# Tokens in groups of 1024 instead of 512: one scan, decay, sigmoid and product over two PSUM banks, late expert weights, late constants

## The chip, the cores and the metric

The kernel runs on one core of one Trainium2 chip. The metric is the device time of the kernel in microseconds (us). The kernel before takes 220.52 us, the median of three runs (220.2 to 220.78). Engines are called by the names of the profile: PE is the matrix engine (TensorE), PEld its weight load, DVE is VectorE, ACT is ScalarE, POOL is GpSimd, SP is SyncE, which here only issues DMAs.

A run is called slow here when it took over 1.5% longer than the fastest run of the same kernel; the others are fast. Ratios compare fast runs with fast runs, and profiles are of fast runs, unless the text says otherwise. A median is of all runs of a kernel.

## The reference, cut to what matters

```python
# x, f_logit: (4, 5056, 256) float32; lower_bound: (256,)
sig = 1 / (1 + np.exp(-f_logit))
f = lower_bound + (1 - lower_bound) * sig
for t in range(S):                       # a recurrence over 5056 tokens, per batch and channel
    h = f[:, t] * h + (1 - f[:, t]) * x[:, t]
    y[:, t] = h
# y as (20224, 256) goes into a soft mixture of 8 experts with 4 slots each
logits = y @ phi                         # phi: (256, 32)
d = softmax(logits, axis=0)              # over all 20224 tokens
slot_in = d.T @ y                        # 32 slots
slot_out[e] = relu(slot_in[e] @ w1[e]) @ w2[e]    # w1: 256 x 1024, w2: 1024 x 256
out = softmax(logits, axis=1) @ slot_out
```

The last line needs the slots of all tokens. So no output can start before the whole input has been scanned, and the kernel has three stages: an input stage (load, gate, scan, logits, slot sums), a short expert stage, and an output stage. The profile counts 58.2 MB read from HBM and 20.7 MB written.

## The kernel before: the parts that matter

A unit is 512 tokens of one batch, and four units (one of each batch) are a group. 5056 tokens are nine groups of 512 and one of 448, which lies on 112 partitions.

```python
R = 4; G = P * R                          # 4 tokens a partition, 512 a unit
def rows(g): return min(P, (S - g * G) // R)
# ... constants: identities, phi scaled by (1 - lower_bound), all before the loop ...
W_AT = {i: 1 for i in range(1, 34, 4)}    # which unit issues how many of the 16 weight loads
W_AT.update({34: 1, 35: 2, 36: 2, 37: 2})
# pools: ld 6 (f_t, x_t), sup 4 (s_t, u_t), apool 6 (decays), hpool 7,
# PSUM: psu 2 (sp and up, one bank each), ptp 1 (hp), plg 1 (logits, two banks), pslot 1

def load(n):      # f_t and x_t, 512 KB each, by nc.sync.dma_start
    ...
    nc.sync.dma_start(out=fs[n][:n_p], in_=f_logit[b, ds(g * G, n_p * R)]...)
def gate(n):      # ACT: s = sigmoid(-f_logit), bf16
    nc.scalar.activation(sts[n][:n_p], fs.pop(n)[:n_p], ACT.Sigmoid, scale=-1.0)
def enter(n):     # POOL: u = s * x
    eng.tensor_tensor(uts[n][:n_p], sts[n][:n_p], xs.pop(n)[:n_p], ALU.mult)
def decay(n):     # ACT, for each half o of the channels, after PE has transposed s into PSUM
    a = apool.tile([P, G], F32, name="a", tag="a")
    nc.scalar.activation(a[:, :T], sp[:, :T, o], ACT.Identity, scale=nomlb[:, ds(o, 1)], bias=1.0)
def scan(n):      # DVE, for each half o
    nc.vector.tensor_tensor_scan(h[:, :T, o], decays.pop((n, o))[:, :T], up[:, :T, o],
        hs[n - B][:, ds(G - 1, 1), o] if n >= B else 0.0, ALU.mult, ALU.add)
def keep_tokens(n):   # PE has transposed h back to tokens (hp); DVE or ACT copies it
    copy = nc.scalar.copy if b == 1 else nc.vector.tensor_copy
def exps(g):      # ACT, once for two groups: table load, Exp, and a table load back for the sigmoid
    nc.scalar.activation(etall[...], lgs[0][:, :T], ACT.Exp, accum_out=csum[:, ds(g, 1)])

for n in range(-AHEAD, n_unit + 6):       # AHEAD = 6, the program order of every engine
    unit(load, n + AHEAD)
    unit(decay, n + 1)
    group(exps, n - 2)
    unit(gate, n + 3); unit(enter, n + 3)
    # ... W_AT weight loads on the GpSimd queue ...
    unit(to_tokens, n - 1); unit(s_to_channels, n + 2); unit(u_to_channels, n + 1)
    group(logits, n - 1)
    unit(scan, n); unit(keep_tokens, n - 1)
    # ... weights to tokens, row sums, slot sums of earlier groups ...
# ... expert stage: first layer (hi_ps), transposes (ht_ps), second layer (so4_ps), slot_out ...
# ... output stage: op = weights @ slot_out; ob = op / row sum (DVE or ACT); DMA of 512 KB ...
```

The softmax here doesn't subtract the row's maximum and nothing guards it: scores larger than these inputs give would overflow.

## Time and profile before

| what (profile of the kernel before) | value |
|---|---|
| span | 218.2 us, granted clock 0.807 |
| last scan ends | 139.97 us |
| slot_out starts (the last step before output) | 160.06 us |
| first output issued | 162.53 us |
| output stage, from slot_out to the end | 58.14 us |

The page's second part cuts the span into 40 slices of 5.5 us, counted from 1 here. The digits are busy tenths; the last line is what the DMA engines moved. These are three lines of the kernel before.

```profile
DVE  0779998909999899989998297533168446465530
...
DMA  6999999999999999999999999992009999999995
GB/s 200 414 413 411 321 415 333 404 413 341 390 381 357 414 318 420 320 417 338 399 317 267 243 232 213 197 213 59 5 23 405 405 405 407 400 405 405 405 356 187
```

The DMA engines are full until slice 27 (148 us), nearly idle for three slices, and full again for the output. In slices 22 to 27 (115 to 148 us) they are busy too, but move little: the last group's loads and the weights are slow for the time that they take.

The view by windows gives busy time per engine in a stretch. Columns: start and end, length, then busy us (and instructions) of PE, PEld, DVE, ACT, POOL, then the granted clock, the DMA share and GB/s.

```profile
60.00:80.00 20.00, 13.32 (x135) 10.71 (x136) 19.27 (x20) 18.93 (x26) 16.01 (x12) 1.00 1.04 368
80.00:100.00 20.00, 12.51 (x112) 9.89 (x110) 19.20 (x21) 18.55 (x26) 17.31 (x13) 1.00 1.03 387
```

Three things are at or near their limit at once here: the DMA engines, DVE (96%) and ACT (94%).

From the starts of the scans in the timeline, 4096 tokens take 23.8 us (58.21 to 81.98 and 81.98 to 105.81). Those are 5.95 us per 1024 tokens.

The DMA view of a stretch counts packets and bytes. The first window lies at 105 to 110 us, where loads of 128 partitions run alone; the second at 120 to 125 us, where the last group's loads of 112 partitions run alone.

```profile
DMA packets 575, 2.09 MB, mean 419 GB/s; under 512 B 64, under 2 KB 64, under 8 KB 575
...
DMA packets 343, 1.22 MB, mean 245 GB/s; under 512 B 44, under 2 KB 44, under 8 KB 343
```

The timeline of the end of the expert stage (start, length, engine, line, operation, count, and in brackets the idle time before it and what ended it) is this.

```profile
158.84 0.42 DVE L393 COPY so_1949<-so_ps 128x256 f32<-128x256 f32 x1 [2.46 <-PE so_ps L387]
160.06 0.48 DVE L396 TENSOR_SCALAR slot_out<-so_ps,rcs 128x256 bf16<-128x256 f32 x1 [0.79 <-PE so_ps L395]
```

From the last scan to slot_out, 20.1 us pass. All weights are there by then and nothing is loaded: this is the gap in the DMA line.

### The profile page before, as it was taken

Reading aid. Unit: us, or ns where it says so; the run is one execution under the profiler, and the core shown is the slowest. Engines: PE = TensorE matmul, PEld = TensorE weight load, DVE = VectorE, ACT = ScalarE, POOL = GpSimd, SP = SyncE. Lnnn points to the kernel's source line nnn. Section 1 sums busy time; section 2 is a strip of 40 time slices with the busy share of each in tenths; the row PEclk is TensorE's granted clock in tenths of the full one; section 3 lists DMA queues with packets and bytes.
Section 4 is the critical chain, followed back from the end, with each engine's and each line's share of the span. In section 5 each row is a group of like instructions: output and inputs, shape, how many; then the busy total and the mean of one; then the engine's idle time right before and its main releaser. Section 6 shows DMA issues by size and latency. Waiting matters only on the chain. (4 is left out here: it accounts for less than half of the span.)

```text
span 218.2 us, 3088 instructions
## 1 busy us (share of the span) xinstructions
PE 133.0 (61%) x1042; PEld 90.8 (42%) x1042; DVE 152.3 (70%) x165; ACT 137.1 (63%) x220; POOL 109.7 (50%) x93
## 2 busy tenths in 40 slices
PE   0386637456664776658573793665958778667600
PEld 0275525355553555556452762432733323223300
DVE  0779998909999899989998297533168446465530
ACT  3499556898889989998787858012034554245520
POOL 1379667359993999969983789742000000000000
PEclk9999999969999999999999589555595555555555
DMA  6999999999999999999999999992009999999995
GB/s 200 414 413 411 321 415 333 404 413 341 390 381 357 414 318 420 320 417 338 399 317 267 243 232 213 197 213 59 5 23 405 405 405 407 400 405 405 405 356 187
DMA packets 19696, 70.76 MB, mean 324 GB/s; under 512 B 2464, under 2 KB 2464, under 8 KB 19680
## 3 DMA queue, kind: packets, MB, share of 16 engines
q1 hardware_dynamic: 17088, 62.14, 74.6%
q0 software_dynamic: 2304, 8.39, 19.2%
q8 instruction: 8, 0.13, 0.2%
q10 hardware_dynamic: 288, 0.03, 0.1%
q14 instruction: 8, 0.07, 0.1%
HBM read 58.23 MB, written 20.71 MB: 362 GB/s over the span
## 5 line engine op out<-in xcount | busy, mean ns | idle before, releaser
L150 POOL TENSOR_TENSOR u_t<-s_t,x_t 128x1024 bf16<-128x1024 bf16 (+1 forms) x39 | 83.4, 2152 | 32.6 <-ACT s_t L144 14.2
L184 DVE TENSOR_TENSOR_SCAN h<-a,h,up 128x512 bf16<-128x512 f32 (+1 forms) x72 | 86.5, 1248 | 0.4 <-PE up L157 0.2
L144 ACT ACTIVATE s_t<-f_t 128x1024 bf16<-128x1024 f32 (+1 forms) x40 | 42.6, 1065 | 18.2 <-DMA f_t<-in_f_logit_dram 18.0
L174 ACT ACTIVATE a<-sp,nomlb 128x512 f32<-128x512 bf16 (+1 forms) x80 | 50.2, 685 | 3.9 <-PE sp L157 3.6
L195 PE MATMUL hp<-ident_f,h 128*128 128x128 f32 (+1 forms) x160 | 30.7, 317 | 34.6 <-DVE ht L204 25.5
L420 ACT ACTIVATE ob<-op,rrow 128x256 f32<-128x256 f32 (+1 forms) x64 | 25.1, 474 | 30.2 <-DVE ob L414 13.1
L414 DVE TENSOR_TENSOR ob<-op,rrow 128x1024 f32<-128x1024 f32 (+1 forms) x24 | 29.0, 1223 | 19.5 <-DMA out_dram<-ob 16.2
L195 PEld LDWEIGHTS hp<-ident_f,h 128*128 128x128 f32 (+1 forms) x160 | 22.6, 208 | 45.5 <-DVE ht L204 34.4
L408 PE MATMUL op<-slot_out,etall 32*128 32x256 bf16 (+1 forms) x160 | 33.9, 379 | 12.4 <-ACT ob L420 7.7
L157 PE MATMUL sp<-ident_f,s_t 128*128 128x128 f32 (+1 forms) x160 | 26.7, 296 | 10.2 <-ACT s_t L144 9.8
L408 PEld LDWEIGHTS <-etall 32*128 32x128 bf16 (+1 forms) x160 | 15.4, 130 | 30.9 <-issue 27.7
L157 PE MATMUL up<-ident_f,u_t 128*128 128x128 f32 (+1 forms) x160 | 26.2, 291 | 2.8 <-POOL u_t L150 2.8
L157 PEld LDWEIGHTS sp<-ident_f,s_t 128*128 128x128 f32 (+1 forms) x160 | 20.5, 155 | 11.9 <-ACT s_t L144 11.0
L157 PEld LDWEIGHTS up<-ident_f,u_t 128*128 128x128 f32 (+1 forms) x160 | 20.5, 153 | 3.4 <-POOL u_t L150 3.3
L204 DVE COPY ht<-hp 128x512 f32<-128x512 f32 (+1 forms) x30 | 20.0, 666 | 1.8 <-PE hp L195 1.8
L243 DVE COPY et<-ep 128x1024 bf16<-128x1024 bf16 (+2 forms) x6 | 3.6, 602 | 15.3 <-PE ep L240 15.3
L184 DVE TENSOR_TENSOR_SCAN h<-a,up 128x512 bf16<-128x512 f32 x8 | 9.1, 1202 | 1.5 <-PE up L157 1.5
L228 ACT ACTIVATE etall<-lg 128x1024 bf16<-128x1024 f32 (+2 forms) x6 | 5.2, 872 | 7.2 <-PE lg L219 7.1
L262 POOL TENSOR_TENSOR rs<-rs 128x128 f32<-128x128 f32 (+6 forms) x18 | 7.9, 442 | 1.4
L144 ACT ACT_TABLE_LOAD x5 | 6.4, 1283 | 3.1 <-PEq L439 1.7
L262 POOL TENSOR_TENSOR rs<-et 128x512 f32<-128x512 bf16 (+2 forms) x6 | 6.0, 998 | 3.8 <-DVE et L243 3.8
L270 PE MATMUL slot_ps<-ht,et 128*32 128x256 bf16 (+1 forms) x160 | 7.4, 314 | 0.6 <-DVE et L243 0.6
(89 smaller groups left out, 92.0 us busy)
## 6 DMA issues: line engine op xcount, KB each, us to landing
f_t<-in_f_logit_dram SPq DMA_DIRECT2D x36, 512.0 KB, 12.5
x_t<-in_x_dram SPq DMA_DIRECT2D x36, 512.0 KB, 12.5
out_dram<-ob SPq DMA_DIRECT2D x36, 512.0 KB, 5.6
f_t<-in_f_logit_dram SPq DMA_DIRECT2D x4, 448.0 KB, 15.6
x_t<-in_x_dram SPq DMA_DIRECT2D x4, 448.0 KB, 16.2
out_dram<-ob SPq DMA_DIRECT2D x4, 448.0 KB, 6.0
w_sb_105<-in_moe_w_dram POOLq DMA_DIRECT2D x1, 512.0 KB, 8.6
w_sb_106<-in_moe_w_dram POOLq DMA_DIRECT2D x1, 512.0 KB, 8.1
```

What stands on the lines that cost most here:

```text
L144: nc.scalar.activation(sts[n][:n_p], fs.pop(n)[:n_p], ACT.Sigmoid, scale=-1.0)
L150: eng.tensor_tensor(uts[n][:n_p], sts[n][:n_p], xs.pop(n)[:n_p], ALU.mult)
L157: nc.tensor.transpose(ps[:, :n_p, r], t[:n_p, r], ident_f[:n_p, :n_p])
L174: nc.scalar.activation(a[:, :T], sp[:, :T, o], ACT.Identity, scale=nomlb[:, ds(o, 1)], bias=1.0)
L184: nc.vector.tensor_tensor_scan(h[:, :T, o], decays.pop((n, o))[:, :T], up[:, :T, o], hs[n - B][:, ds(G - 1, 1), o] if n >= B else 0.0, ALU ...
L195: nc.tensor.transpose(hp[:n_p, r], hw[:, :n_p, r], ident_f)
L204: copy(hts[g][:n_p, b].rearrange("p r d -> p (r d)").bitcast(F32), hps.pop(n)[:n_p].rearrange("p r c -> p (r c)"))
L262: nc.gpsimd.tensor_tensor(dst, part[:, :, :w], part[:, :, ds(w, w)], ALU.add)
L270: nc.tensor.matmul(slot_ps[ds(b * NS, NS), :], et[:n_p, r, b], ht[:n_p, b, r], start=(g == 0 and r == 0), stop=(g == n_grp - 1 and r == R ...
L408: nc.tensor.matmul(op[:n_p, r], ew[ds(b * NS, NS), :, r], slot_out[ds(b * NS, NS), :], start=True, stop=True, skip_group_check=True)
L414: nc.vector.tensor_tensor(ob[:n_p], op[:n_p], rrow[:n_p, g, :, ds(b, 1)].broadcast_to([n_p, R, D]), ALU.mult)
L420: nc.scalar.activation(ob[:n_p, r], op[:n_p, r], ACT.Copy, scale=rrow[:n_p, g, r, ds(b, 1)])
```

## The change

The intent is fewer and larger instructions on the busy engines, fewer token copies on DVE, and an earlier first scan, because some constants are no longer built in front of it. The idle DMA time at the end is to be filled with weights: 12 of the 16 weight loads are issued after the last input. The unit becomes 1024 tokens in two halves of 512. The last group has 960 tokens, on 120 partitions. The pools keep about the bytes that they had, so tiles of twice the size are half as many, and four experts' second-layer weights reuse the input buffers.

```diff
-    G = P * R
+    H = 2
+    W = P * R
+    G = W * H
     def rows(g):
-        return min(P, (S - g * G) // R)
+        return min(P, (S - g * G) // (R * H))
     # constants: ident, rep, phi no longer before the loop; the identity in bf16 by one cast
+    def lb_constants(): ...       # called in the loop at n = -2
+    def other_constants(): ...    # ident, rep, phi; called in the loop at n = 1
-    W_AT = {i: 1 for i in range(1, 34, 4)}
-    W_AT.update({34: 1, 35: 2, 36: 2, 37: 2})
+    W_AT = {8: 1, 13: 1, 15: 1, 16: 1, 17: 2 * E - 4}      # 20 units now
-    ld bufs=6, sup bufs=4, apool bufs=6, hpool bufs=7
+    ld bufs=3, sup bufs=2, apool bufs=3, hpool bufs=6
+    # PSUM: sp and the logits share ONE tile of two banks; up has two; slots and ep share a bank
     def load(n):
+            src = src[b, ds(g * G, n_p * R * H)].rearrange("(h p r) d -> p h (r d)", h=H, r=R)
+            nc.sync.dma_start(out=dst[:n_p, k], in_=src[:, k])           # 1 MB
-    def scan(n):                  # [P, 512] for each half of the channels
+    def scan(n, o):               # [P, 1024] at once where all 128 partitions are used
-        copy = nc.scalar.copy if b == 1 else nc.vector.tensor_copy
+        copy = nc.scalar.copy if h == 0 else nc.vector.tensor_copy
     # the loop: AHEAD 5; gate and enter at n + 2, decay at n + 1
+        u_to_channels(n + 1); decay(n + 1); scan(n, 0)
+        to_tokens(n - 1, 0); keep_tokens(n - 1, 0)
+        exps(g1, logits(g1))                   # every fourth unit
+        scan(n, 1); to_tokens(n - 1, 1); keep_tokens(n - 1, 1)
+        # ... slots ...; s_to_channels(n + 2)
     # expert stage: a PSUM tile for each half of the first layer; the row reciprocal later
     # output: the first two pieces are stored in halves
     # ... cut ...
```

## The prediction

> **What bounds it now.** In the page's 40 slices the 16 DMA engines are full from about 3 to 148 us (58 MB read, inputs and weights), nearly idle until 163 us (15 us), and full again for 20.7 MB of output. In the gap the chain of waits runs through the last row sums, first-layer matmuls (148.1), transposes, second-layer matmuls (ending 158.8) and the first evacuation; the first output is issued at 162.5. VectorE is the second limit: 19.1 to 19.4 us busy of each 20 us between 60 and 120 us.
>
> One thing stands out in the DMA view. 128-partition loads alone move about 420 GB/s, a 4 KB packet taking 0.16 us; the last group's 112-partition loads move about 246 GB/s at 0.27 us (112 to 132 us, where VectorE idles up to 4 us at a time). The output of the same 112 partitions is not slowed.
>
> **What changes, per 1024 tokens.** Scans: the 512 and 448 forms (1263, 1130 ns) give 2.08 ns an element plus 0.2 us, so one 1024 scan is an estimated 2.33 us against 2.53 for two. Token copies on VectorE fall from 1.5 to 1 (0.67 us each). VectorE falls from about 6.1 to 5.4 us per 1024 tokens. The GpSimd product takes about 4.2 us of that. The first scan moves from 12.7 to about 11.4 us; the GpSimd product delays the second to about 19.5 us.
>
> Twelve of 16 weight loads move behind the last input. A weight costs 2.5 us of DMA (213 GB/s written, twice that read), so the last 12 take 30 us. Meanwhile the last scans, slots and first layer run. The DMA gap should shrink from 15 to about 5 us: after the last weight only its matmuls, two small copies, one matmul and half an evacuation remain (about 4 us).
>
> **Where it can be lost.** The last group becomes four units of 120 partitions, 7.9 MB instead of 3.7. The Trainium skill ("DMA: Bandwidth & Descriptors", on why a DMA increments its semaphore by 16) says the engine count is the largest up to 16 that divides the partitions: 15 here, with 8 partitions each. If they run near 390 GB/s (15/16 of full), the last input lands near 112, the weights end near 145, the first output is issued near 149. If the 112-partition slowness carries over (205 to 246 GB/s; the trace cannot say), the group takes 32 to 38 us, the last input lands at 120 to 128, the weights follow after one product (a gap of 5 us), and output starts at 162 to 168: 221 to 227 us. I give the slow branch one third: 8 partitions an engine is what full-rate loads have, 7 is not.
>
> **Prediction: 211 us**, 8 in 10 between 204 and 227. Faster by over 2%: 0.6; within 2%: 0.11; slower: 0.29. The output stage stays DMA-bound, about 55 us.
>
> **Right or wrong in the profile.** Scans of 1024 at 2.3 us; VectorE busy down by about 10 us; DMA gap near 5 us; last product, hence the twelve weights, starting near 112; second-layer matmuls waiting for DMA; output stage unchanged. Above all: GB/s and packet time of the last four units' loads.
>
> **What would make it wrong.** Slow 120-partition loads (above); three input buffers failing to keep DMA full; VectorE waiting each unit for the second token half behind ScalarE's copy (0.3 us, 20 times); logits sharing the decay's only PSUM buffer, stalling each fourth unit.

## More of the kernel before

The page's fifth part, the costliest groups, shows the main work: line, engine, operation, out<-in, shapes, count, then busy us and mean ns of one, then the idle time just before and what ended it.

```profile
L150 POOL TENSOR_TENSOR u_t<-s_t,x_t 128x1024 bf16<-128x1024 bf16 (+1 forms) x39 | 83.4, 2152 | 32.6 <-ACT s_t L144 14.2
L184 DVE TENSOR_TENSOR_SCAN h<-a,h,up 128x512 bf16<-128x512 f32 (+1 forms) x72 | 86.5, 1248 | 0.4 <-PE up L157 0.2
...
L174 ACT ACTIVATE a<-sp,nomlb 128x512 f32<-128x512 bf16 (+1 forms) x80 | 50.2, 685 | 3.9 <-PE sp L157 3.6
...
L204 DVE COPY ht<-hp 128x512 f32<-128x512 f32 (+1 forms) x30 | 20.0, 666 | 1.8 <-PE hp L195 1.8
```

The scan hardly waits (0.4 us in all), nor does DVE's token copy (1.8 us).

## The result, and the profile after

The changed kernel takes 241.31 us, the median of four runs (240.77 to 241.69). The kernel before took 220.36 us in the same rounds (218.98 to 220.78). The ratio is 1.0961 (95% interval 1.0906 to 1.1015): it is 9.6% slower. A ratio here is the mean time of one kernel's fast runs over that of the other's of the same rounds, so it is not quite the ratio of the medians that are quoted. The result is numerically correct.

| us, from the profiles | before | after | difference |
|---|---|---|---|
| last scan ends | 139.97 | 153.54 | +13.6 |
| from there to slot_out | 20.1 | 25.5 | +5.4 |
| from slot_out to the end | 58.1 | 59.9 | +1.8 |
| span | 218.2 | 238.9 | +20.7 |

Two thirds of the loss lie in the input stage, which was to become shorter. These are the lines of the 40 slices (6.0 us each) after the change.

```profile
DVE  0465698886698966986888867722306654645520
...
DMA  6999999995969986999999927999934999999995
GB/s 219 417 410 409 410 410 411 406 407 197 348 229 412 320 298 256 298 219 223 231 252 232 248 50 145 210 215 212 212 66 174 395 404 406 402 405 407 346 340 193
```

DVE, which was at 9 for most of the stage, is now between 5 and 9. Up to slice 9 (54 us) the DMA engines are as full as before. From then on they pause, and from slice 18 (101 us) to slice 23 they look busy but move 219 to 252 GB/s. In slices 25 to 29 the late weights follow at about 212 GB/s written. There are now two gaps instead of one long one: slice 24 (50 GB/s), before the weights, and slice 30 (66 GB/s), behind them.

The costliest groups that answer to those of before are these.

```profile
L158 POOL TENSOR_TENSOR u_t<-s_t,x_t 128x2048 bf16<-128x2048 bf16 (+1 forms) x19 | 78.1, 4108 | 50.8 <-ACT s_t L151 39.6
L199 DVE TENSOR_TENSOR_SCAN h<-a,h,up 128x1024 bf16<-128x1024 f32 (+1 forms) x40 | 74.3, 1884 | 0.3
L188 ACT ACTIVATE a<-sp,nomlb 128x1024 f32<-128x1024 bf16 (+1 forms) x40 | 42.8, 1099 | 32.9 <-PE sp L165 19.5
L215 DVE COPY ht<-hp 128x512 f32<-128x512 f32 (+1 forms) x20 | 13.8, 690 | 26.5 <-PE hp L208 26.5
```

Every engine does its work in the time that was predicted for it, or near it (a 1024-token scan alone is 2.34 us). What is new is in the last columns: ACT's decays waited 3.9 us in all before, and now 32.9 us; POOL waits 50.8 us instead of 32.6; DVE's token copy waits 26.5 us for PE's transpose, where it waited 1.8 us before. DVE was nearly full before; now every engine waits for another.

The view by windows of one group of four full units each (the boundaries are scan starts one group apart) says the same.

```profile
54.00:81.24 27.24, 17.67 (x154) 14.96 (x152) 21.82 (x16) 21.49 (x21) 19.94 (x10) 0.87 0.81 306
81.24:108.60 27.36, 17.78 (x154) 14.97 (x152) 21.86 (x17) 21.60 (x21) 19.27 (x9) 0.88 0.89 264
```

4096 tokens take 27.3 us, where the kernel before takes 23.8 us. DVE is busy for 21.8 us of it (80%), ACT for 21.5 us, PE for 17.7 us, the DMA engines for 81 to 89%. No engine is full, and no single one bounds the stage. The trace points to the order of the steps. The chain of waits shows a stretch of it (start, length, engine, what).

```profile
59.35 1.04 PE bank L267 x16
60.39 1.91 PE sp L165 x8
...
62.33 2.12 ACT a L188 x2
...
64.46 0.59 ACT ht L215
...
65.10 0.76 PE hp L208 x4
...
65.88 0.69 DVE ht L215
66.57 0.33 DVE slot_sb L276
66.90 2.27 DVE h L199
```

Here the engines work one after the other. PE transposes s into the only PSUM tile for it. ACT makes the two decays from it, and only then, in its program order, the token copy of the unit before. That copy frees the only PSUM tile `hp`, so PE can transpose the second half of those tokens. DVE copies it, and only then, in its program order, comes to the next scan. With 512-token units the steps were much the same, but there were six decay buffers instead of three and two PSUM tiles for s instead of one; `hp` was a single tile in both kernels.

This stretch lies at the turn of a group, where ACT makes the exponential and PE the slot sums. DVE's timeline shows how much is lost there. These are its token copies, one for each unit, over one group.

```profile
85.55 0.69 DVE L215 COPY ht<-hp 128x512 f32<-128x512 f32 x1 [1.97 <-PE hp L208]
...
93.16 0.69 DVE L215 COPY ht<-hp 128x512 f32<-128x512 f32 x1 [2.10 <-PE hp L208]
...
98.91 0.69 DVE L215 COPY ht<-hp 128x512 f32<-128x512 f32 x1 [0.23 <-PE hp L208]
...
104.86 0.69 DVE L215 COPY ht<-hp 128x512 f32<-128x512 f32 x1 [0.76 <-PE hp L208]
```

The waits add up to 5.1 us, and 4.1 us of them stand in two of the four units: the first comes behind the exponential, the second behind the slot sums. From copy to copy these two units take 8.0 us (from 77.58) and 7.6 us, the other two 5.7 and 6.0 us. So the ordinary units came near the 5.4 us that the prediction had for all of them.

The timeline of DVE, and of POOL at the same time, shows where the late constants went.

```profile
27.57 0.98 DVE L73 CAST ident<-ident_f 128x128 bf16<-128x128 f32 x1
28.47 0.91 DVE L76 COPY rep<-ident_f 32x128 f32<-32x128 f32 x4
29.39 4.22 DVE L79 TENSOR_SCALAR phi<-phi_f,omlb 128x32 bf16<-128x32 f32 x2
29.48 4.09 POOL L158 TENSOR_TENSOR u_t<-s_t,x_t 128x2048 bf16<-128x2048 bf16 x1 [1.01 <-DMA x_t<-in_x_dram]
...
33.53 4.45 DVE L199 TENSOR_TENSOR_SCAN h<-a,up 128x1024 bf16<-128x1024 f32 x2
```

Scaling phi was two instructions of 238 ns each before. Now the first takes 0.24 us and the second 4.07 us (the view of the tile `phi`): the second begins just after the product on POOL does, and the next scan starts when that product is over. The cast of the identity took 0.98 us, against 0.22 us in consts_first below, and it too ended when a product did (the one before this, at 28.5 us). In all, the constants hold DVE for 6.0 us between two scans.

The waits of the DMA queue on SP (engine and line, what was waited for, us in total, times, longest) name why the loads pause.

```profile
SPq L144 <- POOL u_t L158: 69.9, 16, 7.0
...
SPq L144 <- ACT s_t L151: 26.7, 9, 5.2
```

Before, the two longest entries of the loads' waits were other loads (42.2 and 38.3 us): the queue was full. Now the loads wait for POOL and ACT to free the three input buffers.

The DMA view at 104 to 108 us, where the 120-partition loads run alone:

```profile
DMA packets 235, 0.90 MB, mean 225 GB/s; under 512 B 15, under 2 KB 15, under 8 KB 235
```

They are as slow as those of 112 partitions were: 225 GB/s against 245. The 15 small packets are the end marks of one load, one for each engine that took part.

Last, the end of the expert stage in the timeline.

```profile
174.06 0.40 PE L399 MATMUL so_ps<-x_t,hid 128*32 128x256 bf16 x8 [2.05 <-DMA x_t<-in_moe_w_dram]
...
176.60 0.62 PE L399 MATMUL so_ps<-x_t,hid 128*32 128x256 bf16 x8 [2.14 <-DMA x_t<-in_moe_w_dram]
...
177.27 0.42 DVE L405 COPY so_1605<-so_ps 128x256 f32<-128x256 f32 x1 [5.70 <-PE so_ps L399]
...
179.00 0.48 DVE L408 TENSOR_SCALAR slot_out<-so_ps,rcs 128x256 bf16<-128x256 f32 x1 [1.31 <-PE so_ps L407]
```

The second layer waits for its last weights. They are late because they are issued on POOL's queue behind the last product, and that one starts at 139.26 us.

### The profile page after: what moved, and what is told of

It is laid out like the page before. It is cut to its first block, busy times and chain, and to the rows that moved or that the text cites. A ratio compares the mean times of both kernels' runs of the same rounds, so it can differ in the third digit from the quotient of the medians.

```text
span 238.9 us, 2824 instructions
## 1 busy us (share of the span) xinstructions
PE 144.7 (61%) x1040; PEld 107.2 (45%) x1040; DVE 150.3 (63%) x128; ACT 135.5 (57%) x172; POOL 103.5 (43%) x68
## 3 DMA queue, kind: packets, MB, share of 16 engines
q0 software_dynamic: 2304, 8.39, 17.7%
## 4 chain that ended last, share of the span: by engine, by line
DMA 33%; ACT 22%; DVE 17%; PE 12%; issue 7%; SPq 3%; POOL 2%; ACTq 0%; DVEq 0%; POOLq 0%
DMA out_dram<-ob 12%; ACT a L188 9%; DMA x_t<-in_moe_w_dram 8%; DMA f_t<-in_f_logit_dram 8%; DVE h L199 8%; PE hp L208 5%; DMA w_sb_91<-in_moe_w_dram 5%; ACT ht L215 4%; PE sp L165 4%; ACT ob L432 3%; DVE ht L215 3%; DVE ob L435 3%; ACT s_t L151 3%; SPq L443 3%; DVE phi L79 2%
## 5 line engine op out<-in xcount | busy, mean ns | idle before, releaser
L158 POOL TENSOR_TENSOR u_t<-s_t,x_t 128x2048 bf16<-128x2048 bf16 (+1 forms) x19 | 78.1, 4108 | 50.8 <-ACT s_t L151 39.6
L199 DVE TENSOR_TENSOR_SCAN h<-a,h,up 128x1024 bf16<-128x1024 f32 (+1 forms) x40 | 74.3, 1884 | 0.3
L188 ACT ACTIVATE a<-sp,nomlb 128x1024 f32<-128x1024 bf16 (+1 forms) x40 | 42.8, 1099 | 32.9 <-PE sp L165 19.5
L432 ACT ACTIVATE ob<-op,rrow 128x256 f32<-128x256 f32 (+1 forms) x68 | 26.4, 481 | 34.9 <-DVE ob L435 21.8
L151 ACT ACTIVATE s_t<-f_t 128x2048 bf16<-128x2048 f32 (+2 forms) x21 | 38.5, 1836 | 7.8 <-DMA f_t<-in_f_logit_dram 7.8
L435 DVE TENSOR_TENSOR ob<-op,rrow 128x1024 f32<-128x1024 f32 (+2 forms) x24 | 28.0, 1179 | 22.0 <-DMA out_dram<-ob 17.0
L208 PEld LDWEIGHTS hp<-ident_f,h 128*128 128x128 f32 (+1 forms) x160 | 24.2, 209 | 39.0 <-ACT ht L215 32.2
L215 DVE COPY ht<-hp 128x512 f32<-128x512 f32 (+1 forms) x20 | 13.8, 690 | 26.5 <-PE hp L208 26.5
L165 PEld LDWEIGHTS up<-ident_f,u_t 128*128 128x128 f32 (+1 forms) x160 | 23.8, 174 | 4.8 <-POOL u_t L158 4.8
L199 DVE TENSOR_TENSOR_SCAN h<-a,up 128x1024 bf16<-128x1024 f32 x8 | 17.8, 2273 | 5.9 <-PE up L165 5.9
L215 ACT COPY ht<-hp 128x512 f32<-128x512 f32 (+1 forms) x20 | 11.6, 582 | 8.0 <-PE hp L208 8.0
L267 PE MATMUL bank<-ht,et 128*32 128x256 bf16 (+1 forms) x160 | 8.6, 358 | 5.0 <-DVE et L249 5.0
L260 POOL TENSOR_TENSOR rs<-rs 128x256 f32<-128x256 f32 (+5 forms) x15 | 7.4, 491 | 1.2
L151 ACT ACT_TABLE_LOAD x5 | 6.4, 1283 | 1.7 <-PEq L459 1.7
```

Of the source, the lines that this page charges most:

```text
L151: nc.scalar.activation(sts[n][:n_p, k], fs[n][:n_p, k], ACT.Sigmoid, scale=-1.0)
L158: eng.tensor_tensor(uts[n][:n_p, k], sts[n][:n_p, k], xs[n][:n_p, k], ALU.mult)
L165: nc.tensor.transpose(ps[:, h, :n_p, r], t[:n_p, h, r], ident_f[:n_p, :n_p])
L188: nc.scalar.activation(a[:, :, :n_t], sp[:, :, :n_t, o], ACT.Identity, scale=nomlb[:, ds(o, 1)], bias=1.0)
L199: nc.vector.tensor_tensor_scan(h, a, u, carry, ALU.mult, ALU.add)
L208: nc.tensor.transpose(hp[:n_p, r], hw[:, h, :n_p, r], ident_f)
```

## The experiments

The theory after reading the traces had three parts: too little is in flight at the size of 1024 (A), the late constants cost 6 us (B), the slow 120-partition loads cost their share (C). The rival was that the late weights are to blame (D). Unless a profile is named, all times are medians, and the ratio is to the fast runs of the kernel before of the same rounds. Percentage points of ratio may be added only roughly, and the text says where they do not add.

### Undoing one part each

**consts_first**: the changed kernel with its constants built before the loop.

```diff
+        lb_constants()
+        other_constants()
         for n in range(-AHEAD, n_unit + 4):
-            if n + 2 == 0: lb_constants()
-            if n == 1: other_constants()
```

> The changed kernel with all small constants built on VectorE before the first product, as the kernel before does it, instead of behind the first unit (where they occupy VectorE from 27.6 to 33.5 us, 4.2 us of it the two phi scalings beside a running GpSimd product). Theory 1 (a chain of engine waits with few units in flight sets the pace of the whole input stage): all later scans move up by 4 to 6 us, the twelve late weights too, time 235 to 237 us. Theory 2 (the slow 120-partition loads set the end of the input stage): the head start is absorbed by them, 240 to 241 us. Theory 3 (only the weights queued behind the last input matter): they move only if the last product does, so it follows whichever of the two holds.

Measured: 236.02 us against 220.97, ratio 1.072 (1.0655 to 1.0784). The last scan ends at 147.27 instead of 153.54 us, 6.3 us earlier. In DVE's timeline of this run the phi step is short, as nothing of POOL runs beside it:

```profile
6.38 0.39 DVE L79 TENSOR_SCALAR phi<-phi_f,omlb 128x32 bf16<-128x32 f32 x2 [0.28 <-DMA phi_f<-in_moe_phi_dram]
```

So B is shown: 2.4 points of 9.6. Building the constants late saved nothing: with them in front, the first scan starts at 11.57 us, and in the changed kernel at 11.65 us.

**apool5**: five buffers for the decays instead of three. A buffer holds one half of the channels of a unit, so this is two and a half units instead of one and a half.

```diff
-         tc.tile_pool(name="apool", bufs=3) as apool, \
+         tc.tile_pool(name="apool", bufs=5) as apool, \
```

> The changed kernel with five decay buffers instead of three, nothing else. Theory 1: ScalarE's second decay of a unit no longer waits for the scan that frees its buffer (11.5 us of such waits over 8 times), so the loop scan, decay, token copy, transposes, token copy opens in the ordinary units: VectorE's waits before the token copy shrink from 0.2 to 0.8 us to about nothing in these, time 231 to 237 us. Theory 2: no change, 240 to 242 us, since loads set the end. Theory 3: no change.

Measured: 238.73 us against 220.97, ratio 1.0795 (1.0698 to 1.0892); one of the four runs was slow. The last scan ends at 151.77 us, 1.8 us earlier. A part of A, 1.7 points. In time this is a miss (231 to 237 us were expected), but the waits are as theory 1 had them. These are DVE's token copies of one group in this run.

```profile
80.85 0.69 DVE L215 COPY ht<-hp 128x512 f32<-128x512 f32 x1 [1.84 <-PE hp L208]
...
88.34 0.69 DVE L215 COPY ht<-hp 128x512 f32<-128x512 f32 x1 [1.97 <-PE hp L208]
...
93.77 0.67 DVE L215 COPY ht<-hp 128x512 f32<-128x512 f32 x1
...
98.85 0.66 DVE L215 COPY ht<-hp 128x512 f32<-128x512 f32 x1
```

The ordinary units no longer wait, and a group takes about 25.4 us instead of 27.3 (slot sums in DVE's timeline at 63.62, 88.95 and 114.44). The gain is lost again while the slow last loads come in: the next slot sums stand at 146.62 us, 32.2 us later, where the changed kernel takes 27.3 (121.07 to 148.39) and all3 below, with fast loads, 24.3. So the points understate what the buffers do to the pace.

**full128**: the last group loads 1024 tokens on 128 partitions, as all others do, from 64 tokens further back. Only the load is changed, so the values of the last group are wrong (relative error 0.15); it costs slightly more bytes.

```diff
-                    src = src[b, ds(g * G, n_p * R * H)]
+                    src = src[b, ds(min(g * G, S - G), G)]
-                    nc.sync.dma_start(out=dst[:n_p, k], in_=src[:, k])
+                    nc.sync.dma_start(out=dst[:, k], in_=src[:, k])
```

> The changed kernel with the last group's loads made over 128 partitions (the last 1024 tokens of each sequence, 7 percent more bytes; the values are wrong on purpose, the compute still uses 120 partitions). Theory 2: these loads run at about 410 GB/s and 0.16 us a packet instead of about 222 GB/s and 0.28 us, the last input lands 15 us earlier and the time falls by 8 to 15 us, to 226 to 233 us. Theory 1: the loads speed up the same but the engines do not: only the waits for landed inputs after 105 us go (2.8 us before one product, 2 to 3 before sigmoids), 237 to 240 us.

Measured: 237.55 us against 220.97, ratio 1.0744 (1.0699 to 1.0789). The DMA view in the same window, 104 to 108 us, now reads:

```profile
DMA packets 406, 1.60 MB, mean 399 GB/s; under 512 B 16, under 2 KB 16, under 8 KB 406
```

Sixteen end marks, and 399 instead of 225 GB/s. So it is the form of the loads that makes them slow, 120 partitions instead of 128, and not their place in the program. (Their start address moved with it, by 64 tokens; that was not separated.) By itself the speed of these loads is worth only 2.2 points: the last product starts at 137.30 us instead of 139.26, and the last scan does not move (153.85 us), as the chain of engines holds it. The gain comes behind it, where the weights start earlier: 22.5 us to slot_out instead of 25.5.

**w_even**: the weights of the changed kernel issued evenly during the input stage (the rival D).

```diff
-    W_AT = {8: 1, 13: 1, 15: 1, 16: 1, 17: 2 * E - 4}
+    W_AT = {n: 1 for n in range(5, 17)}
+    W_AT[17] = 4
```

> The changed kernel with one weight load per unit from unit 5 to 16 and four after, instead of four early and twelve behind the last product. Theory 3 (the weights behind the last input cost the time): the time falls to below 225 us. Theory 1: the transfers fill DMA time that is idle now (40 to 100 us), the weights end before they are needed, but the last scan still ends near 153 us and the first layer starts near 165 us, so only the wait for the last weights goes: 4 to 5 us, to 236 to 237 us. Theory 2: inputs of the last group compete with the weights, 240 us or more.

Measured: 246.98 us against 220.97, ratio 1.1211 (1.1157 to 1.1265). It is slower than the changed kernel: the last scan ends at 164.6 us, 11 us later, and only 5.6 us of it come back between the scan and slot_out (19.9 us instead of 25.5). For theory 1 this is a miss, as it expected 236 to 237 us; theory 2 had it right that the weights compete with the last inputs. Until then a group takes 27.3 us as in the changed kernel, and the next one 38.4 us (121.05 to 159.46 between slot sums). So D falls as the main cause: late weights cost 5.6 us at the end and spare 11 us before it. Of the two placements tried, late is the better one.

### Undoing several parts together

**all3**: constants first, five decay buffers and 128-partition loads together (the three edits above; wrong as full128 is).

> The changed kernel with three of the edits run before together: constants first, five decay buffers, last group loaded over 128 partitions (values wrong on purpose); weights as in the change. Alone they gave 5.3, 2.6 and 3.8 us against 241.3. If two limits lie close together in the last group (the engine chain, and the slow loads beside the weights), lifting both gives more than the sum of 11.7: 222 to 227 us. If the gains only add: 229 to 231 us. If one cause covers all three: 234 to 236 us.

Measured: 223.69 us against 219.71, ratio 1.0146 (1.0072 to 1.022). The last scan ends at 140.21 us, as in the kernel before (139.97). The three single gains add up to 6.24 points (2.41, 1.66 and 2.17), and together they gain 8.15. They are not independent: with a shorter chain, the data of the last group is really waited for. What stays is 1.5 points, and no gain of the change is to be seen yet.

**consts_apool**: the first two edits alone, to read the share of the loads between it and all3.

> The changed kernel with constants first and five decay buffers, but its own slow 120-partition loads. Alone the edits gave 5.3 and 2.6 us, and with full-rate loads all three came to 223.7. If the slow loads are a second limit just under the engine chain, they bind as soon as the chain is shorter: 232 to 236 us, so that the loads account for 8 to 12 us of what all three gave together, against 3.8 alone. If the chain alone matters: 226 to 229 us.

Measured: 230.37 us against 220.47, ratio 1.0462 (1.0388 to 1.0536); one of four runs slow. It lies between the two expected ranges. The loads are then worth 3.2 points, about 7 us, between consts_apool and all3, and 2.2 points alone. That is below the 8 to 12 us that one branch expected of them.

**order**: an attempt to mend A by the program order alone. The first half's token transpose and copy go in front of the next gate, and the transposes of s in front of the slot sums.

```diff
+            if has(n - 1): to_tokens(n - 1, 0); keep_tokens(n - 1, 0)
             if has(n + 2): gate(n + 2); enter(n + 2)
...
-            if has(n - 1): to_tokens(n - 1, 0); keep_tokens(n - 1, 0)
...
+            if has(n + 2): s_to_channels(n + 2)
             slots(g2, 0) ...
-            if has(n + 2): s_to_channels(n + 2)
```

> The changed kernel with two places of the emitted order altered and nothing else: the first token half of a unit (its transposes and ScalarE's copy) stands before the sigmoid and the decays of the later units instead of behind them, and the sigmoid transposes stand before the slot matmuls. If VectorE's 26.5 us of waiting before its token copy is head-of-line blocking (the scans behind that copy are ready, but the copy needs transposes that wait for ScalarE's copy, which stands behind sigmoid and decays), these waits fall below 10 us and the unit period from 6.8 to about 5.7 us until the last group; there the slow loads take over, so 230 to 236 us. If buffers or loads and not the order cause the waits: 240 us or more.

Measured: a clear miss. The median is 261.07 us; three of four runs were slow, so no ratio is formed, and the one fast run took 255.93 us, still far above the 230 to 236 us that were expected. The profile, of a slow run, shows the waits in another place:

```profile
ACT ht L215 <- PE hp L208: 59.3, 20, 5.5
...
PE sp L165 <- ACT a L188: 38.4, 13, 3.4
```

ACT now waits 59.3 us for `hp`, because in its own order PE stands at the transposes of s, which wait for the decays to free their only PSUM tile. So this order moved the wait instead of removing it. Whether another order does better was not tried.

### What the exponential does, in both kernels

All exponentials run on ACT, and each turn loads a table for the exponential and one back for the sigmoid (1.28 us each, in both kernels). **no_table** and **b_no_table** put a sigmoid in the place of the exponential, in the changed kernel and in the kernel before, so no table has to be changed. Nine of the ten table loads go; one stays at the start. (The kernel before has six exponentials, not the five of its expectation, for the same ten loads.) The function is then another one; the numbers still pass the tolerance, but this is a probe and not a version.

```diff
-            nc.scalar.activation(etall[...], lg[...], ACT.Exp,
+            nc.scalar.activation(etall[...], lg[...], ACT.Sigmoid,
```

> The changed kernel with the sigmoid function in place of the exponential in the five logit activations (values wrong on purpose), so that ScalarE changes no function tables in the input stage: ten loads of 1.28 us less. If ScalarE lies on the chain that paces the input stage, most of each group's 2.56 us is saved up to the last group: 4 to 11 us, 230 to 237 us. If ScalarE has slack as its 57 percent of busy time suggests: 240 us or more.

> The same edit in the kernel before (its five exponentials become sigmoids, wrong on purpose). If the deeper buffering there hides ScalarE's table loads behind VectorE and the DMA, as the theory has it: 218 to 220.5 us, a gain under 2 us. If they cost there what they cost in the changed kernel, the gain is the same.

Measured: no_table 235.41 us against 220.47, ratio 1.0664 (1.06 to 1.0727; the profiled run was slow); b_no_table 219.51 us, ratio 0.9935 (0.9867 to 1.0003). The same loads are worth 3.0 points in the changed kernel and 0.65 points in the kernel before, where the interval reaches 1. This is A once more: in the kernel before, a turn of the exponential is nearly hidden, and in the changed kernel it is not.

**b_apool3** takes the buffers away from the kernel before: three decay buffers instead of six, one and a half units as in the changed kernel.

```diff
-         tc.tile_pool(name="apool", bufs=6) as apool, \
+         tc.tile_pool(name="apool", bufs=3) as apool, \
```

> The kernel before with three decay buffers instead of six, nothing else. If a ring of three costs in itself: 4 us or more, 224 to 230 us, as ScalarE's second decay then waits for a scan in every unit. If it costs only where a unit is twice as long and ScalarE's copy stands in every unit's loop: 220 to 222 us.

Measured: 226.13 us against 219.39, ratio 1.0252 (1.0176 to 1.0328); one of four runs slow. Six microseconds come from three missing buffers. DVE's timeline says where: this is a turn of the exponential in b_apool3.

```profile
95.82 2.45 DVE L184 TENSOR_TENSOR_SCAN h<-a,h,up 128x512 bf16<-128x512 f32 x2
102.65 0.69 DVE L243 COPY et<-ep 128x1024 bf16<-128x1024 bf16 x1 [4.39 <-PE ep L240]
```

And this is one in the kernel before.

```profile
69.37 2.44 DVE L184 TENSOR_TENSOR_SCAN h<-a,h,up 128x512 bf16<-128x512 f32 x2
72.54 0.69 DVE L243 COPY et<-ep 128x1024 bf16<-128x1024 bf16 x1 [0.73 <-PE ep L240]
```

DVE idles 4.39 us instead of 0.73. The turns come every 27.5 us in b_apool3 (75.12 to 102.65) and every 23.8 us in the kernel before (72.54 to 96.38), for 4096 tokens each. So in this kernel the depth of the decay ring is what hides the exponential, and that can be shown without any 1024-token unit. The run is not the changed kernel in small, though: three buffers of 512 tokens are half the tokens of three buffers of 1024. An estimate from the durations in the traces puts the three kernels side by side. While DVE scans from one buffer of k, the other k - 1 can be full: 5 scans of 1.22 us are 6.1 us of work in the kernel before, 2 of 1.22 us are 2.4 us in b_apool3, and 2 of 2.33 us are 4.7 us in the changed kernel. A turn of ACT without decays takes two table loads, the exponential with its sum (1.2 us) and one sigmoid (1.06 us at 512 tokens, 1.92 us at 1024): 4.8 us in the first two kernels and 5.7 us in the changed one. The ring covers the turn in the kernel before alone. In the changed kernel the same bytes are ahead as before, but one of three buffers is always in use instead of one of six, and the step to be covered has grown.

The estimate is not the whole account. By it, five buffers would cover the turn in the changed kernel too (4 scans of 2.33 us are 9.3 us), and yet all3 loses about 2 us a group to it, as all4x below shows. The trace of all3 names another wait: at 102.67 us DVE's token copy has waited 1.83 us for `hp`. That tile came free only when ACT had made its own token copy at 100.87 us, which in ACT's order stands behind the exponential, the sigmoid and two decays. So the ring is one part of A, and the place of ACT's token copy is another. The second was not tested alone: the run order moved that copy together with another step.

**all4x**: all3 with the sigmoid in the place of the exponential (wrong).

> The changed kernel with constants first, five decay buffers, full-rate last loads (wrong values on purpose) and the sigmoid function in place of the exponential (no table loads). If the rest above the kernel before is ScalarE's chain at the exponentials: a group's period falls from about 25.5 to 23 us or less and the time from 223.7 to 214 to 219 us. If the weights behind the last input hold the end now: 221 to 223 us.

Measured: 214.71 us against 219.39, ratio 0.9773 (0.9723 to 0.9823). The last scan ends at 132.37 us. Relative to all3 this is 3.7 points. With constants, buffers, loads and tables taken out of the way, it is faster than the kernel before. That is no gain of the 1024-token form, though: b_wlate below takes 214.35 us with 512-token units, the exponential and slow last loads, by late weights alone, and its last scan ends at 132.4 us too. A group takes about 23.3 us here, about 25.4 us in all3 (between the slot sums in DVE's timelines: 57.35, 80.72, 103.85, 127.22, and 59.96, 85.45, 110.79), 27.3 us in the changed kernel, and 4096 tokens take 23.8 us in the kernel before.

### Which parts help the kernel before

**b_full128**: the last group's loads of the kernel before on 128 partitions (wrong).

```diff
-                out=fs[n][:n_p],
-                in_=f_logit[b, ds(g * G, n_p * R)]...
+                out=fs[n],
+                in_=f_logit[b, ds(min(g * G, S - G), G)]...     # and the same for x
```

> The kernel before with its last group loaded over 128 partitions instead of 112 (values wrong on purpose). If the partition count alone makes such loads slow: packets of 0.16 us, about 410 GB/s to the end, VectorE's idle time near 120 us gone, the input stage 4 to 6 us shorter, 214 to 217 us. If the slowness came from the addresses or from the weights beside them: no change in packet time, 220 us.

Measured: 217.66 us against 219.71, ratio 0.9888 (0.9833 to 0.9942). The loads run at 421 GB/s at 120 to 123 us, where the kernel before moved 245. The last scan ends at 137.41 instead of 139.97 us. It is a small gain, 1.1 points, and just misses the expected 214 to 217 us.

**b_wlate**: the kernel before with late weights: the part D of the change, alone.

```diff
-    W_AT = {i: 1 for i in range(1, 34, 4)}
-    W_AT.update({34: 1, 35: 2, 36: 2, 37: 2})
+    W_AT = {8: 1, 16: 1, 24: 1, 30: 1, 33: 1, 34: 2, 35: 3, 36: 3, 37: 3}
```

> The kernel before with five weight loads before the last group of inputs instead of nine and eleven behind (the idea of the change's weight placement, alone, without larger groups). If covering the DMA gap with weights is worth what the prediction took it for: inputs land earlier, the first layer starts up to 8 us sooner, the gap of 15 us of idle DMA shrinks to 6 to 9, 212 to 216 us. If VectorE paces the input stage anyway: the last scan moves by 2 to 4 us at most, 217 to 220 us.

Measured: 214.35 us against 219.71, ratio 0.9723 (0.9657 to 0.9789), with correct results. The last scan ends at 132.4 us instead of 139.97. The line of GB/s of its 40 slices (5.3 us each):

```profile
GB/s 205 414 410 409 408 411 408 400 327 414 412 409 332 395 415 409 399 325 420 266 245 266 225 216 213 213 213 200 29 140 405 405 404 402 403 405 408 404 334 192
```

The gap has one slice instead of three. The gain itself lies before it: the last scan is 7.6 us earlier, and from there to slot_out it takes 1.4 us longer than before (21.5 us). At the turn near the last inputs DVE now waits 0.74 us (at 114.76 us), where it waited 4.52 us (at 123.94 us) with more weights under way. So late weights are the part of the change that pays, and they need no large units.

**b_best**: the kernel before with b_wlate's weights; the last group starts 64 tokens earlier and is loaded on 128 partitions (the scan's carry is taken 64 tokens earlier, and the overlapped tokens are kept out of the sums and not stored again, so the result is correct); a PSUM tile for each half of the first layer; the row reciprocal behind the first layer; the first two outputs in halves. The last three come from the change.

```diff
+    def first(g): return min(g * G, S - G)          # where a group's loads start
+    def skip(g): return LAP if g == n_grp - 1 else 0  # LAP = 64 tokens seen twice
-                    hs[n - B][:, ds(G - 1, 1), o] if n >= B else 0.0,
+                    hs[n - B][:, ds(G - 1 - skip(n // B), 1), o] if n >= B else 0.0,
-                nc.scalar.activation(etall[:, ds(gs[0] * G, T)], lgs[0][:, :T], ACT.Exp,
+                nc.scalar.activation(etall[:, ds(gs[0] * G + k, T - k)], lgs[0][:, k:T], ACT.Exp,
+    # etall's first 64 columns of the last group are set to 1e-30; its stores take partitions 16 to 127
```

> A version meant to beat both, correct: the kernel before with eleven weights late (that edit alone gave 214.4), the last group loaded over 128 partitions by starting 64 tokens earlier (the repeated tokens get a weight of 1e-30 and are not written), the first layer's halves in separate PSUM tiles, the large reciprocal moved behind the first layer, and the first two outputs split in halves. The lap should be worth 2 to 4 us, the rest 1 to 3: 208 to 212 us. If the late weights now set the end alone, the lap still frees DMA time for them, 210 to 213.

Measured: 212.37 us (210.36 to 214.72) against 220.47, ratio 0.9614 (0.9543 to 0.9685), correct; one of four runs slow. It beats both kernels. Its last scan ends at 132.47 us as in b_wlate, and slot_out starts 17.7 us later, at 150.13, where b_wlate needs 21.5 us. So the overlap did not move the last scan; the other parts were not separated, and the interval of the ratio still touches that of b_wlate.

**mended**: the changed kernel with constants first, five decay buffers, the same correct overlap of the last group, and eight early weight loads instead of four.

```diff
-    W_AT = {8: 1, 13: 1, 15: 1, 16: 1, 17: 2 * E - 4}
+    W_AT = {8: 1, 10: 1, 11: 1, 12: 1, 13: 1, 14: 1, 15: 1, 16: 1, 17: 2 * E - 8}
+    # and consts_first, apool5, and first(g), skip(g) as in b_best
```

> The changed kernel, correct, with the named causes mended: constants first, five decay buffers, the last group loaded over 128 partitions by starting 64 tokens earlier (repeated tokens weighted 1e-30 and not written), and eight weights instead of four issued before the last input. If the account is complete, it comes to the kernel before or a little under, 217 to 222 us; the exponentials' share of about 4 us stays in it. If something unnamed is left: 224 us or more.

Measured: 225.49 us against 219.39, ratio 1.0234 (1.017 to 1.0298), correct, and a miss: 217 to 222 us were expected. Against all3, which has four weights fewer among the last inputs, the last scan is 3 us later (143.2 against 140.21); slot_out comes 1.8 us earlier (161.99), and the output stage is 62.0 us instead of 60.0. Its last slices but one store at 390, 320 and 298 GB/s, where all3 has 406, 335 and 335. Why that tail is slower stays open.

## Why the prediction was wrong

The prediction was 211 us (204 to 227), and the result is 241.31 us, outside the range and on the other side of the kernel before. Point by point:

1. **The pace of the input stage: the step that failed.** The prediction said "VectorE falls from about 6.1 to 5.4 us per 1024 tokens" and let the input stage follow from that. The work was counted right: DVE is busy for 21.8 us per four units, 5.45 us a unit. But the unit takes 6.8 us. Busy time of one engine was taken for the period, where it is only a lower bound. What came in its place are waits of DVE for a chain through PE, ACT and PE, most of them at the turn of a group. For 4096 tokens DVE works 21.8 us, and the changed kernel takes 27.3 us. With five decay buffers it takes 25.4 us (apool5, and all3, so that constants and loads do not bear on this pace). Without table loads as well it takes 23.3 us (all4x). Of the 1.5 us that remain, the trace shows one wait behind the slot sums, of 1.7 to 2.0 us a group; no run tests it, nor the single PSUM tiles. The kernel before takes 23.8 us with DVE busy for 96% of the time, and has six decay buffers for three units, where the changed kernel has three for one and a half. With three it takes 27.5 us (b_apool3, nothing else changed). The prediction did list "three input buffers failing to keep DMA full" and two stalls among what would make it wrong, but gave none of them a size that counted. The last of them, a stall of each fourth unit, came nearest.

2. **The constants: not costed at all.** The prediction took the earlier first scan as a gain, and it did move from 12.71 to 11.65 us. But consts_first has it at 11.57 us, so the late constants are not the reason. It gave no cost to building the constants between the scans of the second and the third unit: 6.0 us on DVE, of which 4.07 us are one small instruction beside POOL's product. consts_first returns 2.4 points. The Trainium skill ("SBUF — State Buffer", section "SBUF: two separate sides") describes a pair of ports that VectorE and GpSimd share as "an exclusive lock, not a bandwidth split": between a GpSimd instruction and a VectorE instruction of certain kinds (in a fast mode that uses both ports, or with two inputs in SBUF), whichever begins first has it for its whole instruction. The trace agrees with it in time: a 0.24 us instruction took 4.07 us beside a 4.09 us product, and both phi steps together took 0.39 us when nothing ran beside them. Not every VectorE instruction is held: two scans in a row took 4.46 us beside a product (from 39.26 us) and 4.45 us without one (from 33.53 us).

3. **The slow branch of the last loads came.** The prediction gave it one third, for the reason that "8 partitions an engine is what full-rate loads have, 7 is not". That reason was wrong: 120 partitions move 219 to 252 GB/s in the slices where they run, and 225 in the window shown. The count of engines was right. The Trainium skill ("DMA: Bandwidth & Descriptors", section "Why a DMA increments its semaphore by 16 and not by 1") says that the largest number up to 16 that divides the partitions is used, and the trace shows 15 end marks for a 120-partition load and 16 for one of 128. But the rate does not follow from the count: 15 of 16 engines would be 94%, and the loads moved 56% (225 of 399). full128 shows that loads of 128 partitions at the same place are not slow, worth 2.2 points alone and 3.2 points where the chain is shorter. Why fewer partitions are slow was not tested.

4. **The slow branch's own sum was too small too.** It said "the group takes 32 to 38 us, the last input lands at 120 to 128 ... output starts at 162 to 168". The last product started at 139.26 us and the first output at 181.41 us. The pace (1) and the constants (2) were missing in it: consts_apool, which mends the constants and the decay buffers and keeps the slow loads, issues its first output at 170.12 us, near that branch. Both branches shared the wrong pace, and so even the range failed.

5. **The late weights: right in idea, wrong in place.** "The DMA gap should shrink from 15 to about 5 us" came about behind the weights: one slice of about 6 us. The second gap of about as much, before the weights, stood in the slow branch alone ("the weights follow after one product"). Nothing was gained in the changed kernel, because the weights start only after the last product, and that was late. From the last scan to slot_out it takes 25.5 us instead of 20.1. Late weights are shown good by b_wlate (2.8% faster), though by an earlier last scan, and w_even shows that the opposite is worse here.

6. **Smaller terms.** The scan of 1024 elements took 2.33 us, as estimated. Its gain was overstated: two scans of 512 in a row take 2.44 us in the timeline of before, not the sum of 2.53, since they overlap. By the groups, the scans fell by 3.4 us and the token copies by 6.2 us. The total of DVE fell only from 152.3 to 150.3 us, not by 10, as the stalled phi step and the slot sums added to it. The output stage was to stay at about 55 us from the first output on; it went from 55.7 to 57.5 us (218.2 less 162.53, and 238.9 less 181.41). The sentence that the output of the 112 partitions "is not slowed" was a misreading: in windows of 3 us, the kernel before stores 403 to 407 GB/s until 208 us, and 358 and then 322 GB/s over the next 6 us, where mostly and then only its 112-partition tiles are stored. The changed kernel stores 310 to 345 GB/s in the last 16 to 4 us, and has more of such tiles.

The three parts B, C and the buffers of A give back 8.15 of 9.6 points together (all3). The rest of A, the exposed turn of the exponential, is worth 3.7 points at that stage (all4x), which is more than the 1.5 points that were left. (The kernel before would gain 0.65 points of this too, as b_no_table shows.)

Some things stay open. The granted clock was lower in the input stage of the changed kernel (0.87 against 1.00 in the middle of it), and PE's transposes took a little longer (`hp` 327 against 317 ns, `sp` 342 against 296). Over the whole span it is 0.730 to 0.748 in the runs of the changed kernel. In all4x, with fewer waits, it is 0.777 to 0.804, beside 0.790 to 0.808 for the kernel before in the same rounds. So the lower clock goes with the waits, but no run tells whether it is their cause or follows from them. Why loads of 112 and 120 partitions are slow is not settled, and neither is the tail of mended. Whether the 1024-token form could beat b_best with more PSUM and decay buffers was not tried. Five decay buffers did fit (apool5); a second PSUM tile for s or `hp` was not tried.

## What to carry to other kernels

Busy time per unit is a lower bound of the period; before units are made larger, count how many are in flight at each ring of buffers, and follow one unit around the loop through all engines, with each engine's program order. Do this above all at the turns that come only once in several units, as most of the waiting was there. Work that is moved "behind the first unit" lands on the engine that sets the pace, and it may meet another engine there which was not running at the start. A change of many parts should be costed and tried part by part: here one part, late weights, was worth 2.8% alone, while the whole lost 9.6%.

## What the Trainium skill lacked or had wrong

- No page gives the rate of loads to between 64 and 128 partitions: the measured table in "SBUF — State Buffer" has 4, 16, 32, 64 and 128. "DMA: Bandwidth & Descriptors" tells the number of engines, which agrees (15 end marks for 120 partitions), but the rate does not follow from it: 225 GB/s on 120 partitions and 245 GB/s on 112, against 399 to 421 GB/s on 128.
- No page says that stores lose less than loads. Stores moved 322 GB/s where only 112-partition tiles were left (kernel before) and 310 to 345 GB/s with 120 partitions (changed kernel), against 403 to 407 GB/s from 128.
- "SBUF — State Buffer" states the lock for both directions, but works out only the one in which VectorE holds off the descriptors of GpSimd's DMAs. An example of the other would help whoever moves small VectorE work: an instruction of 0.24 us took 4.07 us beside a GpSimd product of 4.09 us.
- "ScalarE: Activation LUTs", section "What ACT_TABLE_LOAD costs", gives about 1283 ns for a load, which agrees (1283 ns mean), and a total of about 2.66 us with a drain for each switch. Here the drain was not to be seen: at 66.13 us in the kernel before the load starts 0.02 us after the decays end, and the exponential starts at 67.43, 1.30 us later.
